# Linear attention and spectral mixing on one core: attention cut into steps with a fixed order on every engine, and twelve weight transfers moved to the start

## The chip, the cores and the metric

The kernel runs on one core of a Trainium2 chip. The metric is device time in microseconds (us), the median of several runs. Executions come in a fast and a slower state. PE is the matrix engine (PEld in the profiles is its loading of weights into the array), DVE the vector engine, ACT the scalar engine. POOL's queue issues the casting transfers (weights, k and q, float32 in memory to bf16 on chip); SP's queue issues the plain ones (v and the outputs).

## The reference, cut to what matters

```python
# q, k, v: (8 batches, 8 heads, 576, 64); w_phi: (64, 128)
def phi(x):
    proj = einsum('bhsd,df->bhsf', x, w_phi)
    proj = proj - max(abs(proj), axis=-1)
    return concat([exp(proj), exp(-proj)])
kv  = einsum('bhsf,bhsd->bhfd', phi(k), v);  z = sum(phi(k), axis=2)
num = einsum('bhsf,bhfd->bhsd', phi(q), kv)
den = einsum('bhsf,bhf->bhs',  phi(q), z) + 1e-6
x = (num / den)                      # as (8, 576, 512)
X = rfft(x, axis=1)[:, :64]          # 64 modes
Y = X times a complex 512x512 matrix per mode    # moe_w_r, moe_w_i: 134 MB of float32
u = x + irfft(Y);  out = u + relu(u @ w_ch)
```

## The kernel before

The kernel does attention in 16 units, each one group of two heads (g = 0 to 3) of one pair of batches (bp = 0 to 3). A unit loads k, q and v, works on its keys, then on its queries, and ends with the forward transform into XT. The weights come in 64 *pairs* (a real and an imaginary half of 512 KB as bf16, for one g and four modes). When the four units of a g are done, the 16 pairs of that g can be *mixed*; a mix frees its pair's buffer. After attention the remaining mixes run together with the channel products (`channels`), then comes the output stage.

```python
pw_cm = tc.tile_pool(name="pw", bufs=7)      # seven buffers for weight pairs
pin_cm = tc.tile_pool(name="pin", bufs=2)    # k, q and v of two units
...
def load(g, bp):                             # k and q on POOL's queue, v on SP's
    for t, src, eng in ((kb, k, nc.gpsimd), (vn, v, nc.sync), (qb, q, nc.gpsimd)):
        ...
def wload(g, mg):
    wt = pw.tile([128, 2, MG, DMODEL], BF16, name="wt", tag="wt")
    for i, w in ((0, moe_w_r), (1, moe_w_i)):
        nc.gpsimd.dma_start(wt[:, i], w[...])
...
for n, u in enumerate(units):
    if n + 2 < len(units):
        st[units[n + 2]] = load(*units[n + 2])
    next_w(2 if g == 0 else 3)               # weight pairs
    if n + 1 < len(units):
        keys(st[units[n + 1]])
    queries(st.pop(u), XTb[g % 2])
    for _ in range(3):                       # three mixes, once a g is complete
        if mixq:
            key = mixq.pop(0)
            mix(*key, wts.pop(key), XTb[key[0] % 2])
    if bp == NP - 1:
        mixq += [(g, mg) for mg in range(NMG)]
...
while mixq:                                  # after attention
    mix(...)
    next_w(1)
    for _ in range(2):
        if todo: channels(*todo.pop(0))
```

The order in which each engine gets its instructions is not the order of this text: a scheduler of the framework chooses it before the kernel is compiled. Once compiled, that order stands.

## Time and profile before

| | before |
|---|---|
| time, median | 547.7 us |
| span of the profiled run | 550.3 us |
| attention | to 365 us (start of the last matmul of the forward transform, rounded down, here and below) |
| unit length | about 20.5 us |
| weight pairs issued / mixes done when attention ends | 42 / 37.6 |
| last mix | 502 us |
| output stage | 48 us |

From the page of the kernel before: the span, the PE's busy time, and three rows of the 40 slices (tenths of the slice that the PE was busy; its granted clock in tenths of full speed; busy share of the DMA engines).

```profile
span 550.3 us, 8008 instructions
...
PE   2377767658667666778768677787766774345995
...
PEclk9999575775675897678975777799989996565899
DMA  9699993343999999999999999799999999995466
```

No engine is saturated. The DMA row is full nearly everywhere, but has a hole in slices 7 to 10. The table of stretches gives it numbers (stretch in us, its length, busy time and instructions of PE, weight loads, DVE, ACT and POOL, then clock, DMA share and GB/s); a share of about 1.24 to 1.28 is a full queue.

```profile
core 0: us, PE busy (x) PEld busy (x) DVE busy (x) ACT busy (x) POOL busy (x), PEclk, DMA share, GB/s
502.40:550.30 47.90, 38.98 (x161) 15.56 (x163) 25.01 (x37) 22.29 (x38) 0.00 (x0) 0.86 0.53 203
364.00:502.40 138.40, 85.68 (x562) 37.35 (x566) 25.39 (x51) 29.55 (x51) 34.08 (x46) 0.82 1.22 208
84.00:134.00 50.00, 34.93 (x330) 24.20 (x333) 29.95 (x52) 29.97 (x46) 12.47 (x19) 0.67 0.33 53
```

Between 84 and 134 us all seven weight buffers are full and nothing can be mixed yet. From 364 to 502 us the DMA queue is full, and the kernel goes at the pace of the weights.

Two lines of the view of waits (engine, what it issued, what released it, us in total, times, longest): the weight issues wait for mixes 37 us, and loads of k hardly hold the PE (these 5.7 us are at the start of the program; no line has the PE waiting for q).

```profile
POOL wt L327 <- PE one L344: 37.4, 5, 17.0
...
PEld L172 <- DMA kb<-in_k_dram: 5.7, 2, 5.2
```

And two lines of the view of transfers, for issues at 141.3 to 141.7 us (size, us from issue to landing). This q load was issued behind eight weight halves, and landed together with the last of them, 20.6 us later. In the hole between 84 and 134 us the same view has 3.2 us for such a q.

```profile
wt<-in_moe_w_i_dram POOLq DMA_DIRECT2D x1, 512.0 KB, 20.7
qb<-in_q_dram POOLq DMA_DIRECT2D x1, 128.0 KB, 20.6
```

### The profile page before, as it was taken

The numbers are of one execution on the slowest core, as the hardware profiler recorded it, in microseconds if no ns is written. First come the engines' busy times: TensorE is split into PE (matmuls) and PEld (weight loads), VectorE is DVE, ScalarE is ACT, GpSimd is POOL, SyncE is SP. The second block draws the span as 40 slices with busy tenths as digits, with TensorE's granted clock in tenths as the row PEclk, the third lists the DMA queues.
The fourth block names the chain that finished last, engine by engine and source line by source line (L and its number), as shares of the span: only waits on it lengthen the run. The fifth ranks groups of instructions, "written<-read, shape, count | busy, mean of one in ns | idle before, by whom it ended". The sixth has DMA issues, their size and how long they took to land.

```text
span 550.3 us, 8008 instructions
## 1 busy us (share of the span) xinstructions
PE 376.5 (68%) x3103; PEld 221.7 (40%) x3133; DVE 279.7 (51%) x486; ACT 256.5 (47%) x403; POOL 186.8 (34%) x273
## 2 busy tenths in 40 slices
PE   2377767658667666778768677787766774345995
PEld 1255545445445444455445354343333331111342
DVE  7647485584555764566965665662222220000574
ACT  3346555655565566567665565312221331011463
POOL 8853331133432715626242533143223222200000
PEclk9999575775675897678975777799989996565899
DMA  9699993343999999999999999799999999995466
GB/s 166 87 225 204 215 140 60 64 49 65 206 189 210 135 218 178 160 213 180 214 218 215 181 181 184 117 204 206 206 206 206 212 216 213 215 213 99 163 267 267
DMA packets 112341, 98.63 MB, mean 179 GB/s; under 512 B 17968, under 2 KB 110768, under 8 KB 111280
## 3 DMA queue, kind: packets, MB, share of 16 engines
q0 software_dynamic: 94736, 77.09, 90.0%
q1 hardware_dynamic: 17568, 21.04, 12.6%
q8 instruction: 24, 0.39, 0.3%
q14 instruction: 13, 0.11, 0.1%
HBM read 163.64 MB, written 9.44 MB: 314 GB/s over the span
## 4 chain that ended last, share of the span: by engine, by line
PE 41%; DMA 23%; ACT 18%; DVE 12%; issue 4%; POOL 2%; DVEq 0%; POOLq 0%; ACTq 0%
DMA wt<-in_moe_w_i_dram 15%; DMA wt<-in_moe_w_r_dram 8%; PE two L186 7%; PE one L230 6%; ACT AQ L263 5%; PE one L236 5%; PE one L344 5%; ACT AB L211 4%; PE pt L466 3%; ACT AB L212 3%; PE one L283 3%; DVE mk L189 3%; PE one L312 3%; PE pt L468 3%; ACT qT L173 2%
## 5 line engine op out<-in xcount | busy, mean ns | idle before, releaser
L327 POOL DMA_DIRECT2D wt<-in_moe_w_r_dram x64 | 48.9, 764 | 93.3 <-PE one L344 37.4
L263 ACT ACTIVATE AQ<-two 128x1024 bf16<-128x1024 f32 x64 | 61.6, 1027 | 14.8 <-PE two L186 6.1
L327 POOL DMA_DIRECT2D wt<-in_moe_w_i_dram x64 | 49.0, 765 | 48.7 <-DMA wt<-in_moe_w_i_dram 44.7
L81 POOL DMA_DIRECT2D kb<-in_k_dram x32 | 23.6, 736 | 78.4 <-PE one L283 32.7
L394 ACT CAST xw<-one 128x512 bf16<-128x512 f32 x36 | 21.1, 585 | 62.0 <-PE one L392 54.9
L230 PE MATMUL one<-va,AB 128*128 128x65 bf16 x512 | 48.2, 231 | 2.6 <-DVE va L219 2.6
L392 PE MATMUL one<-wchb,xT 128*128 128x512 bf16 x137 | 39.7, 408 | 13.9 <-DVE xT L389 13.5
L186 PE MATMUL two<-w2blk,qT 128*128 128x256 bf16 x128 | 30.2, 386 | 26.4 <-ACT qT L173 26.3
L211 ACT ACTIVATE AB<-two 128x1024 bf16<-128x1024 f32 x32 | 32.9, 1028 | 31.4 <-DVE mk L189 24.6
L283 PE MATMUL one<-kvz,AQ 128*128 128x65 bf16 x512 | 35.2, 226 | 15.5 <-ACT AQ L263 13.8
L344 PE MATMUL one<-wt,XT_70 128*32 128x512 bf16 x256 | 28.7, 524 | 24.1 <-DMA wt<-in_moe_w_i_dram 14.4
L189 DVE TENSOR_REDUCE mk<-two 128x8 f32<-128x1024 f32 x32 | 42.1, 1493 | 4.7 <-PE two L186 4.7
L389 DVE COPY xT<-one 128x512 bf16<-128x512 bf16 x36 | 15.3, 424 | 56.4 <-PE one L387 56.3
L219 DVE TENSOR_TENSOR va<-vn,ee 128x1152 bf16<-128x1152 f32 x32 | 42.0, 1356 | 0.0
L189 DVE TENSOR_REDUCE mq<-two 128x8 f32<-128x1024 f32 x32 | 38.9, 1218 | 4.2 <-PE two L186 4.0
L283 PEld LDWEIGHTS <-AQ 128*128 128x128 bf16 x512 | 28.8, 120 | 28.4 <-ACT AQ L263 22.9
L312 PE MATMUL one<-CF,xs 128*128 128x256 bf16 x160 | 30.0, 309 | 13.1 <-DVE xs L303 12.1
L81 POOL DMA_DIRECT2D qb<-in_q_dram x32 | 23.4, 731 | 43.5 <-PE two L172 24.3
L230 PEld LDWEIGHTS <-AB 128*128 128x128 bf16 x512 | 32.4, 119 | 10.5 <-issue 3.2
L212 ACT ACTIVATE AB<-two 128x1024 bf16<-128x1024 f32 x32 | 33.0, 1032 | 0.0
L344 PE MATMUL one<-wt,XT_69 128*32 128x512 bf16 x256 | 26.5, 465 | 7.0 <-DMA wt<-in_moe_w_i_dram 5.8
L172 PE MATMUL two<-ident_b,kb 128*128 128x128 bf16 x144 | 18.1, 280 | 19.0 <-DVE ident_b L107 8.4
(136 smaller groups left out, 716.5 us busy)
## 6 DMA issues: line engine op xcount, KB each, us to landing
wt<-in_moe_w_r_dram POOLq DMA_DIRECT2D x64, 512.0 KB, 14.5
wt<-in_moe_w_i_dram POOLq DMA_DIRECT2D x64, 512.0 KB, 16.2
vn<-in_v_dram SPq DMA_DIRECT2D x32, 256.0 KB, 6.7
out_dram<-of SPq DMA_DIRECT2D x8, 1024.0 KB, 3.9
kb<-in_k_dram POOLq DMA_DIRECT2D x32, 128.0 KB, 5.5
qb<-in_q_dram POOLq DMA_DIRECT2D x32, 128.0 KB, 5.8
vn<-in_v_dram SPq DMA_DIRECT2D x32, 32.0 KB, 7.3
XT_69<-yst SPq DMA_DIRECT2D x8, 128.0 KB, 6.1
```

Source lines behind the costliest of these rows:

```text
L81: eng.dma_start(t[:, 8 * i:8 * i + 8, :].rearrange("p (h c) d -> p h (c d)", h=2), hs[:, 0:512, :].rearrange("h (p c) d -> p h (c d)", c=4),)
L186: nc.tensor.matmul(o, lhsT=tT[:, 4 * i + j, :], rhs=w2blk.rearrange("p (c f) -> p c f", c=2), start=True, stop=True)
L189: nc.vector.tensor_reduce(out=m[:, 8 * i:8 * i + 8], in_=ps, axis=AX.X, op=ALU.max, apply_absolute_value=True,)
L211: nc.scalar.activation(dst[:, 0], ps, ACT.Exp, scale=1.0)
L212: nc.scalar.activation(dst[:, 1], ps, ACT.Exp, scale=-1.0)
L219: nc.vector.tensor_tensor(out=va[:, ab, :, 0:64], in0=st["vn"], in1=ee[:, ab, :].unsqueeze(2).to_broadcast([128, 18, 64]), op=ALU.mult,)
L230: nc.tensor.matmul(o, lhsT=ABs[i][:, ab, 4 * h + c, :], rhs=va[:, ab, 8 * i + 4 * h + c, :], start=(c == 0), stop=False,)
L263: nc.scalar.activation(AQ[:, ab], ps, ACT.Exp, scale=1.0 - 2.0 * ab)
L283: nc.tensor.matmul(pn[ab][:, n - n0, :], lhsT=AQs[i][:, ab, c % 2, 2 * h + c // 2, :], rhs=kvz[:, i, 2 * h + ab, :], start=True, stop=True,)
L312: nc.tensor.matmul(px[:, :, i, :], lhsT=xs[:, g, bp, n:n + 2, :].rearrange("p h d -> p (h d)"), rhs=CF[:, c if c < 4 else 4 + i], start=(c ...
L327: nc.gpsimd.dma_start(wt[:, i], w[mg * MG:(mg + 1) * MG, g * 128:(g + 1) * 128, :].rearrange("m p e -> p m e"),)
L344: nc.tensor.matmul(py[32 * j:32 * j + 32, :], lhsT=XT[:, s0:s0 + 4, :, 32 * t + 4 * o + j].rearrange("p r b -> p (r b)"), rhs=wt[:, i, j, ...
```

## The change

The intent is threefold. Attention becomes 17 steps; step n does the queries of unit n and the keys of unit n+1, woven piece by piece. Every instruction of attention is pinned behind the one written before it on its engine, also on POOL's and SP's queues. And weight pairs land early, thirteen instead of seven before the first mix: eight buffers instead of seven, and five pairs of g = 0 in places that are not in use yet (two in the accumulator `yacc`, one in the second XT, two in the attention result `xs`).

```diff
+class InOrder:                                # wraps an engine
+        def call(*args, **kwargs):
+            ins = f(*args, **kwargs)
+            return self.tc.keep_in_program_order(ins) if self.on else ins
...
+    pe, dve, act = (InOrder(tc, e) for e in (nc.tensor, nc.vector, nc.scalar))
+    pool, sp = InOrder(tc, nc.gpsimd), InOrder(tc, nc.sync)
...
-    pw_cm = tc.tile_pool(name="pw", bufs=7)
+    pw_cm = tc.tile_pool(name="pw", bufs=8)
...
+    def home(g, mg):
+        if g == 0 and mg < 2:
+            t = yacc.bitcast(BF16)...
+        elif g == 0 and mg == 2:
+            t = XTb[1]...
+        elif g == 0 and mg in (10, 11):
+            t = xs[:, mg - 8]...
+        else:
+            return pw.tile([128, 2, MG, DMODEL], BF16, name="wt", tag="wt")
...
+    for n in range(-1, len(units)):
+        K = units[n + 1] ...;  Q = units[n] ...;  L = units[n + 3] ...
+        W = (2, 3, 3, 3)[n + 1] if n < 3 else 3              # weight pairs
+        X = 0 if n < 4 else 6 if n == 4 else 2 if n % 2 else 4   # mixes
+        K.turn_k()                  # PE transposes k of unit n+1
+        L.load_k()                  # k of unit n+3
+        Q.cols_q(0); Q.exp_q(0)
+        next_w(1)
+        K.rows_k(0); K.exp_k(0)
+        Q.cols_q(1); Q.num(0)
+        some(X // 2)                # the middle mixes
+        K.turn_q()                  # PE transposes q of unit n+1
+        L.load_q()
+        Q.exp_q(1)
+        K.rows_k(1); K.exp_k(1)
+        Q.num(6); Q.cols_q(2); Q.exp_q(2)
+        K.rows_k(2); K.exp_k(2); K.weigh_v(); K.rows_q(0); K.weigh_v2()
+        L.load_v()
+        next_w(W - 1)
+        Q.num(12)
+        K.rows_q(1); K.rows_q(2); K.exp_mq()
+        some(X - X // 2)            # the late mixes
+        K.kv(0); K.kv(1); Q.freq()
...
+    for e in (pe, dve, act, pool, sp):
+        e.on = False                # after attention the scheduler is free again
```

(Cut: the guards `if K`, `if Q` and `if L`, the bodies of the steps, which are the old code in pieces, and the tables' new scratch space. The transposes' copy is done in two parts, some tiles of attention and two after it have other numbers of buffers, the clearing of XT moves from POOL to DVE, and the loads of a unit are written two steps before their use instead of one.)

## The prediction

> **What bounds it now.** By the page no engine is saturated (PE 68%). By the table of stretches, three stages. Attention, 20 to 360 us: sixteen units, about 20.5 us each, a chain through all engines. Then 364 to 502 us: DMA share 1.22, the chain of waits mostly weight transfers, 5.1 us for each of the last 27. Then 48 us of output. Between 84 and 134 us the DMA share is only 0.33: the seven weight buffers are full. The share summed to 502 us is 540; at 1.24 throughout, 436 us: 65 us of DMA time idle.
>
> **What the change does.** Thirteen weight pairs instead of seven can land before the first mix (eight buffers, and borrowed space in yacc, XT and xs). By the end of attention 46 pairs are loaded (now 37); 18 remain, 91 us instead of 138. Were that all, I would say 490 to 515.
>
> **Step length.** In the fixed order I follow one chain, with durations from the timeline: from the second query exponential, numerator (0.6), DVE numerators, row maxima and weighted values (10.2), e2 and kvz copies (1.0), px copy (0.7), key copies (1.2), exponentials (2.0), cols, num and mix (2.6), query turn and copies (1.6), exponentials (2.0): 21 to 22 us with mixes, 20.4 without. Weaving, I estimate, shortens no unit.
>
> **The new wait.** The POOL queue is fixed too, and this I hold decisive. From step 8 on, weight pair w needs the buffer of mix w-8. Loads of k and q of unit n+3 stand behind pairs 3n+3 and 3n+4. For even steps, the queries that the PE turns right after the middle mixes were queued behind a pair that waits for exactly those mixes. Transfers land in queue order: a q issued behind eight weight halves took 20.6 us to land, one with an idle queue about 3. (The Trainium skill, "DMA: Bandwidth & Descriptors", section "SWDGE vs HWDGE vs iDMA", has each DMA engine drain its ring packet by packet; the trace agrees.) Into an idle queue the first half landed after 5.5 us, the second, issued 0.75 later, after 7.3; plus 2.2 for q: 10.6 us from mix to data. Exposed: about 10 us for q in every even step, 4 us for k in every step. Two steps take 62 us (before: 40).
>
> **Sum.** Step 0 starts near 22 us, inverse tables cost about 5; step 8's middle lies near 206; three pairs of steps bring step 14's middle to about 395. From there 22 pairs remain to land: 135 us, to 530. Then 48: span about 578; recorded times were 2 us less. I lean downward, as my chain may be pessimistic: 572 us, range 525 to 608. Chances: faster by over 2% 0.2, within 2% 0.13, slower 0.67.
>
> **Shown right or wrong by:** DMA share above 1.1 from 20 to 105 us, low afterwards; in the waits, PE transposes waiting for kb and qb landings, over 50 us together (now under 10), and POOL's weight issue for PE mixes; PE idle 10 us in even steps from step 8; unit length 20 to 22 us before step 8, about 31 after; the stage of DMA alone 90 to 100 us; the end 48 to 50.
>
> **What would make it wrong.** A step of 17 to 18 us (I may have misordered ACT and DVE): about 530. Small loads landing ahead of weights: about 510. The clock: PE idling may lower it (the skill's "TensorE: Matmul & The Clock Gate", "HAM oscillation"; here 0.67 in 84 to 134, 0.86 at the end), 10 us.

## The result, and the profile after

The changed kernel takes 606.0 us (604.9 to 607.1) against 547.7 us: the ratio is 1.106, with a 95% interval of 1.101 to 1.110. It is slower by 10.6%. Ratios here and below are the mean time of one kernel's fast runs over that of the other's of the same rounds, so not quite the ratio of the medians.

The same rows of the page:

```profile
span 603.1 us, 8011 instructions
...
PE   3666766766766638575466538583787777743895
...
PEclk9977567668688565565576565657679999995798
DMA  9999999139997766975997786987799999998276
```

The early transfers do what they should: the DMA row is full in the first seven slices. But the hole only moved (slices 8 and 9), and from slice 13 to 29 a new one lies over the whole of the second half of attention. In the table of stretches:

```profile
20.00:105.00 85.00, 58.91 (x515) 41.44 (x519) 55.73 (x109) 49.32 (x82) 38.76 (x56) 0.72 1.27 208
105.00:130.00 25.00, 17.51 (x168) 11.68 (x168) 18.00 (x29) 13.15 (x24) 0.41 (x1) 0.70 0.10 25
216.90:283.00 66.10, 38.77 (x310) 23.75 (x308) 27.81 (x44) 26.31 (x43) 20.22 (x29) 0.55 0.87 140
283.00:349.00 66.00, 37.89 (x314) 23.48 (x312) 29.17 (x47) 25.45 (x42) 19.47 (x28) 0.60 0.83 132
349.00:411.90 62.90, 39.63 (x326) 23.96 (x323) 29.87 (x49) 25.77 (x43) 19.50 (x29) 0.58 0.82 129
450.30:556.00 105.70, 71.74 (x527) 32.93 (x535) 23.17 (x47) 29.51 (x51) 25.55 (x35) 0.93 1.21 206
556.00:603.10 47.10, 38.09 (x161) 15.33 (x163) 25.21 (x37) 22.57 (x38) 0.00 (x0) 0.86 0.54 206
```

The three stretches of about 66 us are two steps each, in which neither the DMA queue nor any engine is full. The view of waits names what holds them:

```profile
POOL wt L38 <- PE one L38: 247.1, 28, 32.6
...
PE one L38 <- DMA qb<-in_q_dram: 35.5, 9, 8.7
...
PE one L38 <- DMA kb<-in_k_dram: 34.4, 13, 5.8
```

(All pinned instructions have line 38, the helper's.) The weight issues now wait for mixes 247 us instead of 37, and the PE waits 70 us for k and q (8 us of these for the very first k; 62 us from step 8 on). The two are one loop. The timeline of the POOL queue over one such wait:

```profile
197.92 0.74 POOL L38 DMA_DIRECT2D wt<-in_moe_w_r_dram  x1 [7.46 <-PE one L38]
198.65 0.75 POOL L38 DMA_DIRECT2D wt<-in_moe_w_i_dram  x1
199.39 2.64 POOL L38 DMA_DIRECT2D kb<-in_k_dram  x4
216.90 0.77 POOL L38 DMA_DIRECT2D wt<-in_moe_w_r_dram  x1 [14.87 <-PE one L38]
217.65 0.75 POOL L38 DMA_DIRECT2D wt<-in_moe_w_i_dram  x1
218.39 2.64 POOL L38 DMA_DIRECT2D qb<-in_q_dram  x4
```

The four parts of a q load need no weight buffer, and their own buffer had come free two steps earlier (its last reader, the transpose of the q of two units before, stands at 167 us). But they stand behind a weight pair. That pair waits 14.9 us until a mix has freed a buffer, and only 1.5 us after it does the q load start. This load was needed at once: the PE, done with the step's mixes, stands idle for 8.4 us and transposes this q at 225.8 us, as it lands. The PE's timeline shows the same meeting one turn of the loop (two steps) later:

```profile
276.50 1.46 PE L38 MATMUL one<-ident_b,kb 128*128 128x128 bf16 x9 [3.09 <-DMA kb<-in_k_dram]
...
281.70 0.87 PE L38 MATMUL one<-kvz,AQ 128*128 128x65 bf16 x12
282.50 1.96 PE L38 MATMUL one<-wt,XT_70 128*32 128x512 bf16 x16
292.49 0.61 PE L38 MATMUL one<-ident_b,qb 128*128 128x128 bf16 x4 [8.03 <-DMA qb<-in_q_dram]
```

The middle mixes (`wt,XT_70`) free the buffers, and the very next thing in the PE's fixed order is the transpose of a q that was queued behind those buffers: 8 us of idleness, and by the fixed order nothing else may fill it. The starts of the key transposes in the timeline give the length of the steps: 21.2 to 21.5 us in steps 1 to 3, about 22 in steps 5 and 6, and from step 8 on 67.0, 66.2 and 62.9 us for each two.

### The profile page after: what moved, and what is told of

The parts are those of the page before. It is cut to its first block, busy times and chain, and to the rows that moved or that the text cites. A ratio compares the mean times of both kernels' runs of the same rounds, so it can differ in the third digit from the quotient of the medians.

```text
span 603.1 us, 8011 instructions
## 1 busy us (share of the span) xinstructions
PE 392.5 (65%) x3104; PEld 229.1 (38%) x3133; DVE 287.5 (48%) x492; ACT 261.0 (43%) x435; POOL 181.7 (30%) x267
## 5 line engine op out<-in xcount | busy, mean ns | idle before, releaser
L38 POOL DMA_DIRECT2D wt<-in_moe_w_r_dram x59 | 44.9, 761 | 266.2 <-PE one L38 247.1
L38 POOL DMA_DIRECT2D wt<-in_moe_w_i_dram x59 | 44.6, 755 | 33.0 <-DMA wt<-in_moe_w_i_dram 30.5
L38 POOL DMA_DIRECT2D qb<-in_q_dram x64 | 42.2, 671 | 36.6 <-DMA wt<-in_moe_w_i_dram 19.3
L38 POOL DMA_DIRECT2D kb<-in_k_dram x64 | 42.3, 677 | 12.9 <-PE one L38 6.3
L38 PE MATMUL one<-ident_b,kb 128*128 128x128 bf16 x144 | 18.7, 297 | 34.8 <-DMA kb<-in_k_dram 34.4
L38 PE MATMUL one<-ident_b,qb 128*128 128x128 bf16 x144 | 16.4, 274 | 35.7 <-DMA qb<-in_q_dram 35.5
L38 ACT COPY qT<-one 128x512 bf16<-128x512 bf16 (+1 forms) x32 | 19.6, 645 | 44.4 <-PE one L38 44.3
L38 PE MATMUL two<-qT,w2blk 128*128 128x512 bf16 x48 | 21.6, 514 | 24.1 <-ACT AQ L38 21.1
L38 PE MATMUL one<-CF,xs 128*128 128x256 bf16 x160 | 36.5, 412 | 0.0
L38 PE MATMUL one<-wt,XT_70 128*32 128x512 bf16 x256 | 28.5, 543 | 11.0 <-DMA wt<-in_moe_w_r_dram 5.5
```

Source lines behind the costliest of these rows:

```text
L38: ins = f(*args, **kwargs)
```

## The experiments

All 14 kernels of the experiments gave correct results. Runs of the kernel before on the same chip: medians 548.3 (e1 to e4), 548.1 (e5, e6, e8, e9), 546.4 (e10 to e13) and 550.5 us (e14, e15). Pairs issued (to about half a pair) and the end of attention are counted in each timeline. Against the kernel before, e2, e3, e9 and e14 are faster by an interval that leaves out 1 but not the 2% that counts here as clearly faster; against the changed kernel, at 1.106, e1 to e3, e5, e6 and e10 to e13 are all clearly faster.

| run | POOL and SP | compute engines | other edit | time, us | ratio to before | PE's waits for k and q | attention ends | pairs issued by then |
|---|---|---|---|---|---|---|---|---|
| changed kernel | fixed | fixed | – | 606.0 | 1.106 | 69.9 | 450 | 47 |
| e1 | free | fixed | – | 529.9 | 0.968 | 8.6 | 373 | 47 |
| e2 | fixed | free | – | 541.9 | 0.988 | 59.4 | 380 | 47.5 |
| e5 | free | free | – | 495.6 | 0.904 | 11.4 | 327 | 46 |
| e3 | fixed | fixed | pairs issued right after mixes | 532.2 | 0.973 | 2.6 | 378 | 47 |
| e10 | fixed | fixed | q one pair earlier | 571.1 | 1.047 | 38.9 | 421 | 46.5 |
| e12 | free | PE free | – | 529.2 | 0.968 | 10.4 | 374 | 47 |
| e13 | free | DVE and ACT free | – | 514.3 | 0.941 | 9.8 | 361 | 47 |
| e6 | fixed | fixed | e3 with 4 mixes a step | 507.6 | 0.925 | 6.9 | 374 | 53.5 |
| e11 | free | free | no borrowed places | 509.4 | 0.932 | 19.2 | 345 | 46.5 |
| e4 | kernel before | | early pairs | 551.6 | 1.008 | | 365 | 42 |
| e9 | kernel before | | 4 mixes a step | 537.4 | 0.980 | | 395 | 51.5 |
| e8 | kernel before | | early pairs, 4 mixes a step | 530.8 | 0.963 | | 385 | 52 |
| e14 | fixed | fixed | e3, PE waits filled | 536.3 | 0.974 | 9.1 | 380 | 46.5 |
| e15 | fixed | fixed | PE waits filled | 598.7 | 1.084 | 56.5 | 446 | 46.5 |

The theory (A): the fixed transfer queue puts loads of k and q behind weight pairs that wait for mixes, and the PE then waits for the loads. The main rival (B): the fixed order of the compute engines is what costs.

**e1: the transfer queues left to the scheduler.**

```diff
+    pool.on = sp.on = False
     const = ctx.enter_context(tc.tile_pool(name="const", bufs=1))
```

> The changed kernel with the POOL and SP queues left to the scheduler (the three compute engines stay in the fixed order). The scheduler then issues the k and q loads of steps 4 to 15 well ahead of the weight pairs that wait for mixes. Theory A (the fixed transfer queue holds k and q behind weights that wait for mixes): the PE's waits for kb and qb, 70 us in the changed kernel, fall under 15, steps 8 to 15 fall from 33 to about 22 us, time 520 to 545 us. Rival B (the fixed order of the compute engines is the loss): time stays above 585 us.

Measured: 529.9 us, the waits for k and q 8.6 us, steps of 22 us to the end. As A expected. (This frees SP too; e3 below leaves SP fixed and gains as much, so SP's order is not needed for the gain.)

**e2: the compute engines left to the scheduler, the queues fixed.**

```diff
+    pe.on = dve.on = act.on = False
     const = ctx.enter_context(tc.tile_pool(name="const", bufs=1))
```

> The changed kernel with PE, DVE and ACT left to the scheduler and POOL and SP in the fixed order. Theory A: the waits for kb and qb stay (over 50 us), time 580 to 610 us. Rival B: time falls below 560 us.

Measured: 541.9 us. Here A missed, and B's number came. Yet the waits that A is about are still there, in the view of waits of e2:

```profile
POOL wt L38 <- PE one L38: 181.7, 26, 16.3
...
PE one L38 <- DMA qb<-in_q_dram: 34.1, 10, 7.8
...
PE one L38 <- DMA kb<-in_k_dram: 25.3, 5, 8.1
```

The PE waits 59 us for k and q, nearly as long as the 70 before, but two steps take 52 us instead of 66 (key transposes at 218.9, 270.6 and 323.2 us). So neither theory alone is right. The wait comes from the queue; what a loop through it costs is the wait plus the compute work that the fixed order strings between the load and the next mix. That other work fills the waits in the free order is how I read it; the trace shows only that the loop is 14 us shorter. Nor are the 64 us that e2 saves all the loop's: where POOL is free, freeing the compute engines saves 34 us as well (e1 to e5).

**e3: everything fixed, but each pair issued after the mix that frees its buffer.** This changes only where weights stand in the POOL queue during attention.

```diff
     def some(n):
                 mix(*key, wts.pop(key), XTb[key[0] % 2])
+                if key not in ((0, 0), (0, 1), (0, 2), (0, 10), (0, 11)):
+                    next_w(1)
...
-        W = (2, 3, 3, 3)[n + 1] if n < 3 else 3
+        W = (2, 3, 3, 3)[n + 1] if n < 3 else 0
```

> The changed kernel, all engines still in the fixed order, but from step 3 on each weight pair is issued right after the mix that frees its buffer, instead of two steps earlier in the queue. Only the place of weight transfers in the POOL queue differs. Theory A: waits of PE for kb and qb under 10 us, every step 21 to 23 us, attention ends near 390 us instead of 451, time 525 to 545 us. Rival B: above 585 us. Rival C (the low tensor clock alone, independent of waits): mean clock stays at 0.72 and time above 570.

Measured: 532.2 us. Two lines of its view of waits:

```profile
PE one L38 <- DMA kb<-in_k_dram: 2.4, 1, 2.4
...
PE one L38 <- DMA qb<-in_q_dram: 0.2, 1, 0.2
```

This is the cleanest proof of A: with the order of the compute engines unchanged, the 62 us of waits from step 8 on are gone (the 2.4 us left are the first k of the program) and the time falls by 74 us. The other 12 us are not accounted for; the clock alone (rival C) did not hold the time above 570. Attention ended at 378 us, a little earlier than expected.

**e4: the kernel before with the early pairs alone** (seven buffers and the five borrowed places; the tables' scratch space moved as in the change; cut: the mixes of unit 4 stand before its queries, and the second XT is cleared later).

```diff
+    def home(g, mg): ...      # as in the change
-        wt = pw.tile([128, 2, MG, DMODEL], BF16, name="wt", tag="wt")
+        wt = home(g, mg)
...
-        next_w(2 if g == 0 else 3)
+        next_w(3)
```

> The kernel before with only the early weight transfers added: seven buffers and five borrowed places, twelve pairs before the first mix, order left to the scheduler. If the early transfers are worth what the DMA hole shows: DMA share between 84 and 134 us rises from 0.33 to over 0.9, attention still ends near 360 us, five more pairs are loaded by then (5 x 5.3 us), time 515 to 530 us. If the space is given back later (the queue idles elsewhere instead): 540 to 550 us.

Measured: 551.6 us, ratio 1.008: a miss, also of the second expectation by a little. The hole is filled and comes back later, as two stretches of e4 show:

```profile
84.00:134.00 50.00, 33.92 (x325) 21.85 (x326) 32.17 (x56) 28.27 (x44) 23.07 (x33) 0.76 1.00 155
134.00:184.00 50.00, 34.84 (x329) 23.83 (x328) 29.33 (x48) 29.76 (x48) 20.20 (x29) 0.68 0.74 117
```

In the kernel before, the DMA share of the two was 0.33 and 1.12. In both kernels attention ends at 365 us with 42 pairs issued. The number of pairs that can have been issued by then is at most the number of mixes done plus the number of buffers, and the early transfers change neither. This is theory D, tested next. It gives a ceiling, and the counts stay up to about 3 below it: 42 of 44.6 (37.6 mixes and seven buffers) here and in the kernel before, 47 of 48 (40 mixes and eight buffers) in the changed kernel.

**e5: the changed kernel with all five engines left to the scheduler.**

```diff
+    pe.on = dve.on = act.on = pool.on = sp.on = False
```

> The changed kernel with all five engines left to the scheduler: the fourth cell of the table whose others are the changed kernel (606), POOL free (530) and compute free (542). If the fixed transfer queue and the fixed compute order are two separate costs: compute free saves 2 us in each step without waits, so 15 steps from 530 give 495 to 515 us, with waits for kb and qb under 15 us. If the compute order matters only through the loop of waits (mix, weight pair, load, turn): 525 to 535 us, as with POOL free.

Measured: 495.6 us, 9.6% faster than the kernel before and the best of all. Its stretches:

```profile
20.00:327.00 307.00, 238.30 (x2371) 161.31 (x2401) 213.99 (x370) 196.57 (x332) 138.97 (x200) 0.79 1.21 198
327.00:444.30 117.30, 75.42 (x528) 33.76 (x536) 22.79 (x47) 29.46 (x51) 26.66 (x36) 0.89 1.22 209
```

The DMA queue is nearly full from the start to the last weight; a step takes 18.3 us on average from step 8 on (the key transposes stand at 187.99 and 297.95 us, six steps apart). So all of the loss, and 52 us more, comes from fixing the order; the rest of the change is good. Of what is good, e11 below prices the borrowed places; the other 37 us or so (the eighth buffer, the earlier loads, the woven text as the scheduler gets it) were not taken apart. The two fixed orders are not two separate costs that add up: freeing POOL alone saves 76 us, freeing the compute engines alone 64, freeing both 110.

**e6: e3 with four mixes in a step**, and three channel blocks instead of two after each later mix.

```diff
-        X = 0 if n < 4 else 6 if n == 4 else 2 if n % 2 else 4
+        X = 0 if n < 4 else 6 if n == 4 else 2 if n == 7 else 4
```

> The kernel of e3 with four mixes in a step instead of three on average (all 48 mixes that can be done by then, instead of 38, lie in the attention stage; three channel blocks instead of two after each later mix, so that all are done). Theory D (what counts is the number of weight pairs issued when attention ends, which is mixes done plus buffers): 56 pairs instead of 47 by then, a step longer by 1 us, time 500 to 515 us. Rival (the PE is full, so mixes moved into attention lengthen it by what they save later): 525 to 540 us.

Measured: 507.6 us, attention ends at 374 us as in e3, with 53.5 pairs issued instead of 47. Theory D holds; the extra mixes cost no visible time in attention. The 25 us gained are less than 6.5 pairs at 5.3 us: from 430 to 462 us the DMA share is only 0.79, so the weights are no longer the limit at the end.

**e8 and e9: the kernel before with four mixes and four pairs in a step, with (e8) and without (e9) the early pairs** (cut: three channel blocks after each later mix, as in e6).

```diff
-        for _ in range(3):
+        for _ in range(4):            # mixes in a step
```

> The kernel of e4 (before plus twelve early pairs, 552 us) with four mixes and four pairs in a step instead of three. Theory D: the early pairs are now used, pairs issued at the end of attention rise from 42 to 55, time 505 to 525 us. Rival (early transfers are worth nothing in this kernel for another reason, or DMA contention stretches attention): above 535 us.

> The kernel before, without early pairs, with four mixes and four pairs in a step. Against e8 it prices the early transfers where something uses them. Theory D: the DMA hole between 84 and 134 us stays, the queue is full from 134 us on and attention is slowed by it; 10 to 25 us slower than e8, so 520 to 545 us.

Measured: 530.8 and 537.4 us. Pairs issued by the end of attention rise from 42 to 52 in both, and both are faster than the kernel before. But e8 missed its range: 52 pairs came instead of 55, and attention stretched to 385 us. The early pairs are worth 8 us here (fast runs alone), less than the 10 that I expected; and as the pairs issued are the same in both, this gain is not theory D's count but an attention that ends 10 us sooner.

**e10: one move, q in front of one weight pair.**

```diff
-        next_w(1)
         K.rows_k(0); K.exp_k(0)
...
         L.load_q()
+        next_w(1)
```

> The changed kernel, all engines in the fixed order, with one move in the POOL queue: the q load of unit n+3 stands before weight pair 3n+4 instead of behind it; k stays where it is. Theory A, in its parts: the wait for q (35.5 us in all, about 10 us in each even step from 8 on) goes, the waits for k (34 us, about 4 in each step) stay; two steps take 56 instead of 66 us, time 565 to 585 us. If the loads only have to come two steps earlier as a whole: no change, above 595 us.

Measured: 571.1 us. The waits for q fall from 35.5 to 0.4 us, those for k stay, at 38.5 us, and the time falls by 35 us. Two steps take 58 us (expected 56). This prices the two halves of the loop separately, as predicted.

**e11: e5 without the borrowed places.**

```diff
     def home(g, mg):
-        if g == 0 and mg < 2: ...
+        return pw.tile([128, 2, MG, DMODEL], BF16, name="wt", tag="wt")
```

> The kernel of e5 (all engines free, 496 us) without the five borrowed places: all weight pairs in the eight buffers. Theory D': where the DMA is full all through attention, a hole cannot be filled later, so the five missing pairs cost 5 x 5.3 us: 515 to 525 us, and the DMA share between 80 and 130 us falls below 0.8. If the early transfers do not matter here either (as in e4): 494 to 502 us.

Measured: 509.4 us, between the two expectations: the early transfers are worth 13.8 us here, half of the 26 that five pairs would take. The DMA share between 70 and 130 us is 0.76, against 1.23 in e5.

**e12 and e13: which compute engine's order costs.** Both start from e1; e12 frees the PE too, e13 frees DVE and ACT too.

```diff
+    pe.on = pool.on = sp.on = False            # e12
+    dve.on = act.on = pool.on = sp.on = False  # e13
```

> The kernel of e1 (POOL and SP free, 530 us) with the PE free too; DVE and ACT stay in the fixed order. If the PE's order is what keeps a step at 22 us instead of 18 to 19: 495 to 505 us. If it is the order on DVE and ACT (the chain of copies and maxima that the prediction followed): 520 to 532 us.

> The kernel of e1 with DVE and ACT free too; the PE stays in the fixed order. The mirror of e12. If the PE's order keeps the step at 22 us: 520 to 532 us. If the order on DVE and ACT does: 495 to 505 us. Both between 505 and 520: each contributes.

Measured: 529.2 and 514.3 us, against 529.9 with only POOL free and 495.6 with all free. Freeing the PE alone does nothing; DVE and ACT bring 16 us; all three together 34. So the order on DVE and ACT holds the step first, and a free PE order pays only once they are free (19 us more); e13 fell in its range for "each contributes". One visible piece of that order: in each step ACT waits 6.6 us for the last of the query maxima on DVE (`e_ <- DVE mq` stands 14 times with 6.6 us in the waits of the changed kernel), with the copies of kv behind it.

**e14 and e15: the clock.** The prediction's step was too short, 20.4 us without mixes against a measured 21.4. In the trace, the clock is at half in the last 11 us of a step (81 to 92 us: mean 0.50), and kv and freq take 4.65 and 2.32 us there. I had used durations of the full clock. The end of step 2, from the timelines of PE and then ACT, shows where it enters:

```profile
90.75 2.32 PE L38 MATMUL one<-CF,xs 128*128 128x256 bf16 x10
...
90.81 0.64 ACT L38 CAST kvz<-one 128x260 bf16<-128x260 f32 x2
93.11 0.59 ACT L38 CAST XT_69<-one 128x512 bf16<-128x512 f32 x1 [1.67 <-PE one L38]
```

My chain has ACT go from the copies of kv (kvz) straight to the copy of px (into XT_69). Here ACT waits 1.67 us in between for freq (CF,xs). In e14 (described next) freq takes 1.27 us in step 8, which ends with the clock at 1.00, and this wait of ACT is 0.82 us in steps 8, 10 and 12, which end at a high clock; in the same steps of e3, which have the same mixes and end at half clock, it is 1.87 us. So about 1 us of it goes with the clock, as much as the step was too short. Both runs add useless matmuls, overwritten by the real ones, at two places where the PE waits: e14 to e3, e15 to the changed kernel.

```diff
+        def warm(self, o, n, times):
+            for _ in range(times):
+                pe.matmul(o, lhsT=w2blk[:, 0:128], rhs=CF...[:, 0:n], start=True, stop=True)
...
                 pn[ab] = one([128, 6, 65])
+                if n0 == 6 and ab == 1: self.warm(pn[ab]..., 390, 6)
...
             pk = one([128, 4, 65])
+            if i == 0: self.warm(pk..., 260, 6)      # not for unit 0
```

> The kernel of e3 (532 us) with twelve useless matmuls in each step: six into the numerator's PSUM tile before the real ones overwrite it, six into the kv tile, both at places where the PE waits 1 to 2.3 us for ACT or DVE. Clock theory: the mean granted clock in attention rises from 0.70 to over 0.85, the last part of a step (kv and freq) falls from 7.0 to about 4.5 us, steps fall from 22.4 to about 21.3, time 512 to 522 us. Chain theory (ACT and DVE set the step whatever the clock): 529 to 540 us.

> The changed kernel (606 us) with the same useless matmuls. Clock theory: the clock between 217 and 412 us rises from 0.58 to over 0.7, two steps take 63 to 64 instead of 65 us, steps before 8 about 1 us less, time 585 to 597 us. Chain theory: 602 to 615 us.

Measured: e14 536.3 us, ratio to before 0.974, the same as e3's 0.973. Taken alone that looks like the chain theory. But the clock rose (0.82 instead of 0.70 between 205 and 370 us), and not everywhere. The last 7 us of steps 8 to 10, in e14:

```profile
224.90:231.90 7.00, 5.91 (x68) 3.99 (x61) 5.67 (x9) 0.86 (x3) 3.00 (x4) 0.89 1.29 210
249.00:256.00 7.00, 7.00 (x56) 4.84 (x55) 3.01 (x6) 0.97 (x3) 0.00 (x0) 0.50 1.28 218
270.10:277.10 7.00, 5.86 (x72) 4.18 (x65) 5.66 (x9) 0.86 (x3) 3.00 (x4) 0.95 1.30 208
```

The steps that end at a high clock took 21.6, 21.2 and 22.6 us (8, 10 and 12), those that end at half clock 24.0, 24.2 and 23.9 us (9, 11 and 13). In e3 the same stretches are at 0.50 in all these steps, and the steps take 22.1 to 22.8 us. The useless matmuls before kv often came too late (their tile in PSUM, the memory that matmuls write, was not free before: in step 9 they start at 248.58 us, after 2.85 us of waiting for DVE), so they lengthened the step where the clock stayed low, and the two effects cancelled in the total. The high-clock and low-clock steps also differ in the number of mixes, four against two, so the within-run comparison is not free of that; but the steps with more work are the shorter ones. In e15 the changed kernel gained some: 598.7 us, ratio 1.084 instead of 1.106, just above the range that the clock theory gave. But its waits for k and q also fell, from 70 to 56.5 us, so this gain is not shown to be the clock's. I take the clock as a true part of the miss, about 1 us in a step by the waits of ACT above (an estimate), and its exact share in the total as open.

## Why the prediction was right or wrong

The direction and the mechanism were right; the size was not. Predicted were 572 us, 4.4% slower; measured were 606, 10.6% slower, near the upper end of the range of 525 to 608. The step that failed is the sum: its stretches before the loops and after them, and the 6 us taken off at the end, were set too short. The loops themselves, the heart of the argument, were nearly right.

- **The hole and the early transfers.** Predicted: DMA share above 1.1 to about 105 us. Measured: 1.27 from 20 to 105 us. Right. But "46 pairs are loaded (now 37)" promised 9 pairs more. By the bytes that POOL's queue still moved after attention (26.5 MB from 366 to 502 us in the kernel before, 19.9 MB from 450 to 556 us in the changed one; a pair is 1.05 MB), 38.7 and 45.1 had landed, a gain of 6.4; counted by issues it is 42 and 47, a gain of 5. And e4 shows that the early transfers by themselves give nothing in the old order: the pairs issued by the end of attention are set by mixes and buffers.
- **The step.** "21 to 22 us with mixes, 20.4 without": measured about 22 (24.9 in step 4, which has six mixes) and 21.4. The term that the chain lacks is the wait of ACT for freq at the end of a step, 1.67 us with the clock at half; about 1 us of that goes with the clock (the same steps of e14 and e3).
- **The new wait.** "Exposed: about 10 us for q in every even step, 4 us for k in every step": measured 8 to 8.7 us for q in the even steps, and 3 to 5.5 us for k in most steps from 8 on. e3 and e10 confirm the cause. What the prediction did not see is that the fixed compute order is needed too for the loss: with it free, the same waits cost far less (e2).
- **The sum.** The terms, predicted and measured: middle of step 8 at 206 and 217 us; middle of step 14 at 395 and 412; last landing at 530 and 556; span 578 and 603. The 25 us are thus 11 before the middle of step 8, 6 in the loops (two steps were set at 62 and took 65.4 on average) and 9 after the middle of step 14, less 1 at the end. Of the 11, 2.8 lie before step 0 (it started at 24.8 us instead of 22), 3 in steps 1 to 3 and about 3 in the six mixes of step 4. The 9 come from the stage of DMA alone: set at 91 us (18 pairs at 5.1), it took 105.7. Some 18.9 pairs were still to land, and the same full queue, at 206 GB/s, also carried 1.84 MB of SP's transfers, by my estimate 9 us, so a pair took 5.6. (From the middle of step 14 to the end of attention it took 38 us, less than the 44 that the sum had left (135 less 91), though the DMA share between 412 and 443 us was only 0.93.)
- **The lean.** I took 6 us off the sum, 4 of them because "my chain may be pessimistic"; it was optimistic. The other 2, "recorded times were 2 us less", was a misreading: the profiled run of the kernel before had a span of 550.3 us and a time of 552.1, so times are 2 us *more*. Both errors together are 9 of the 34 us (the profiled run was 1 us faster than the median).
- **The end.** 48 us predicted, 47.1 measured; fewer buffers there cost nothing.

## What to carry to other kernels

A queue that is held in program order should not have a transfer that waits for a buffer in front of one that does not: issue a buffer's next load right behind the work that frees it, and prefetches that need no such buffer stay ahead (e3 gained 74 us by that alone). Fixing the order of all engines at once removes the slack that hides such waits, so free one group at a time to see which order costs (here 606 us with all fixed, 530 with POOL and SP free, 542 with the compute engines free, 496 with all free). And earlier transfers pay only if something downstream can use the room: count the pairs issued when the stage ends before crediting them.

## What the Trainium skill lacked or had wrong

- "TensorE: Matmul & The Clock Gate", section "HAM oscillation — how this bites in real kernels", gives the rule that the PE must have no idle gaps above about 3.4 us. In the changed kernel the clock was at half from 81 to 92 us and averaged 0.63 between 52 and 92 us, although the PE's longest wait in that time was 2.3 us and it was busy 27.6 of the 40 us: keeping to the rule did not keep the clock up in this chain of small matmuls with many short waits. (The page's next section, "A second HAM failure mode: psum-queue depth-cycling", tells of the same from micro-idling in another kernel; neither says how much idling in all is too much.) (That there are two states, half and full, as its section "What's actually happening" says, agrees: stretches of 1 us show 0.50 or 1.00, with 0.95 or 0.96 only at the changes.)
- The same page does not say what a falling clock does to a fixed order. Between e14's steps that ended at 0.89 to 1.00 and those that ended at 0.50 to 0.52 lay 1.3 to 3.0 us in 21 to 24, though they also differ in the number of mixes.
- "DMA: Bandwidth & Descriptors", section "Anatomy of one DMA — SWDGE (gpsimd) path", fits 2.0 us plus bytes over 436 GB/s. For the casting halves here (1 MB read, 512 KB written) that is an estimate of 4.4 us by the bytes read or 3.2 us by those written; the first one into an idle queue took 5.3 to 5.5 us. The page does not say which bytes count for a cast.
- That a transfer lands behind everything issued before it on POOL's queue fits the same page, section "SWDGE vs HWDGE vs iDMA" (each DMA engine drains its ring packet by packet), and the trace agrees (20.6 us behind eight halves, 3.2 us with a queue mostly idle). The section on the SWDGE path says that the issuing sequencer does any waiting before a transfer is dispatched; but no page draws the consequence that such a wait holds back unrelated loads behind it; e3, which removed it, gained 74 us.
